# Shorter filler products at the start, and one mantissa moved behind an activation, in a Fourier mixing and hardswish MLP kernel

## The chip, the core and the metric

The kernel runs on one core of a Trainium2 chip. The metric is the device time of one execution in microseconds (us). The engines are named as the profile names them: PE is TensorE (matrix products), PEld its weight loads, DVE is VectorE, ACT is ScalarE, POOL is GpSimd and SP is SyncE, which issues DMAs.

## The reference

```python
def _attn_ref(x):                       # x: (8, 3008, 256)
    X = np.fft.fft(x, axis=1)
    X = np.fft.fft(X, axis=2)
    return X.real.astype(np.float32)

def _moe_ref(x, w_in, w_out):           # x: (24064, 256), w_in: (256, 2048), w_out: (2048, 256)
    h = x @ w_in
    relu6 = np.clip(h + 3.0, 0.0, 6.0)
    g = h * relu6 / 6.0
    return (g @ w_out).astype(np.float32)
```

The input x is float32, the weights are float64. The real part of a two-dimensional Fourier transform of each of 8 batches goes, flattened to 24064 rows, through a two-layer MLP with the hardswish activation.

## The kernel before

**The long part.** The transform along the sequence (3008 = 47 x 64) is done in two stages, and the transform along the 256 columns is folded into `w_in`, so that the MLP's first products (L558, tiles `u` and `v`) finish the transform too. Work goes by pair of batches, chunk of rows and eight steps (`fc`) in each chunk. A step has the first products (`mlp1`), an activation on DVE and ACT (`activate`: two `s` on L567, a sum and a difference on L577 and L579, `relu` on ACT, and two gates on L609), and the second products with the mixed `w_out` (L653, or L633 in the first chunk). The loop at L1156 issues step s + 2's first products before step s's second ones; what has to be prepared for later chunks is put beside the steps by a table written out by hand. Each engine works through its own instructions in the order in which the program issues them.

**The start.** Before the loop three things are made on the core. The weights arrive as float64 and are converted by hand in 16 pieces of 128x512: `exponent_a` on ACT takes the exponent bytes of a piece into `PM`, `exponent_b` turns them into a power of two by two float16 products with a small table in `FI` (L779), `exponent_c` on ACT finishes that, `mantissa` on DVE makes the fraction by two instructions (L787 and L792), and `join` multiplies the two (L803 or L809). `fold_w_in` (L834) multiplies converted pieces of `w_in` by the column table `C`. In the same stretch the first batch is transformed in its first stage: DVE folds four tiles and their mirrored partners (`fold_columns`, L204 and L205), and PE multiplies each tile and partner by a table of 47 rows and 64 columns (`unit_columns` L342, `unit_middle` L328), on four quarters of the array at a time. Results go by ACT (the last by DVE, L354) to SBUF and on.

**The filler.** Before any data is there, `keep_awake(4)` multiplies a tile of zeros (`Z`) by a tile of ones, both set by DVE. Each float32 product is issued as two passes of 128x512, each with a weight load. It is the first work of PE; behind it come the two exponent products of piece 0 (L779), which wait for `PM`, then `keep_awake(1)` and `keep_awake(1, TB)`, whose results nobody reads either, and then the first tile's `unit_columns`.

**The first eight steps.** While the pieces are still being converted, the loop runs `first_steps` and `second_steps` in turn. In `second_steps(3)`, the fourth step, pieces 10 to 13 are in work: piece 13's `exponent_a` is followed by its `head_b`, which is its `mantissa` (and, for pieces 4 to 9 alone, the issue of a later load), then by half of the second products, then by `mlp1` of the next step, whose activation follows on DVE. Piece 13's `join` comes in the step after that.

Of the kernel before, what the change touches and what calls it, by code (L numbers as in the profile page):

```python
# [7 lines left out]
F32 = mybir.dt.float32  # L8
# [4 lines left out]
F16 = mybir.dt.float16  # L13
# [45 lines left out]
def kernel(  # L59
# [10 lines left out]
    nc = tc.nc  # L70
    P = nc.NUM_PARTITIONS
# [16 lines left out]
    TB = KC * N2  # L88
# [18 lines left out]
    ps_d = ctx.enter_context(tc.tile_pool(name="ps_d", bufs=1, space=PSUM))  # L107
# [20 lines left out]
    ones = consts.tile([P, P], F32, name="ones")  # L128
# [416 lines left out]
    def mlp1(ch, fc):  # L545
        activate(ch, fc, *mlp1_products(ch, fc))
# [64 lines left out]
    def combine(ch, fc):  # L611
        a = ch.a[fc][:].rearrange("p m f n -> p (m f) n")[:, :, 0:ch.n]
        c = cpool.tile([P, 4, TB], F32, tag="c", name="c")
        cn = c[:, :, 0:ch.n]

        eng = nc.vector if ch.final and fc == NF - 1 else nc.gpsimd
        add(cn[:, 0:2], a[:, 2:3].to_broadcast([P, 2, ch.n]), a[:, 3::-3], eng)
        add(cn[:, 2], cn[:, 0], a[:, 0], eng)
        add(cn[:, 3], a[:, 1], cn[:, 2], eng)
        ch.c[fc] = cn  # L620
# [6 lines left out]
    def mlp2_first(ch, fc, halves=(0, 1)):  # L627
        a = ch.a[fc]
        for h in halves:
            if fc == 0:  # L630
                ch.acc[h] = ps_a.tile([P, 2, TB], F32, tag="acc", name="acc")
            for f in range(2):
                nc.tensor.matmul(ch.acc[h][:], G[:, (B11, B12, B21, B22)[2 * f + h], fc, :], a[:, :, f],  # L633
                                 start=(fc == 0 and f == 0), stop=(fc == NF - 1 and f == 1))
            if fc == NF - 1:
                if h == 0:
                    ch.r = epool.tile([P, 2, 2, TB], F32, tag="r", name="r")
                for m in range(2):
                    nc.scalar.mul(ch.r[:, m, h], ch.acc[h][:, m], (1 - 2 * m) / WS)
# [99 lines left out]
    PIECES = [q for j in range(NWO) for q in [("in", j, 0), ("in", j, 1), ("out", j, 0), ("out", j, 1)]]  # L739
# [6 lines left out]
    def load_w(j, queue=nc.gpsimd, clear=None):  # L746
        kind, n, i = PIECES[j]

        pool, tag, bufs = (wpool, "st", 2) if j in STRAIGHT else (spool, "t", None) if j in (2, 3) else (xpool, "x", None)
        st = pool.tile([P, 2 * WB], I32, tag=tag, bufs=bufs, name="st")  # L750
        if clear:
            clear.memset(st[0:1, 0:1], 0)
        o = st[:].bitcast(moe_w_in.dtype).rearrange("p (c j) -> p c j", c=2)
        fs = slice((2 * n + i) * 2 * P, (2 * n + i + 1) * 2 * P)
        if kind == "in":
            queue.dma_start(out=o, in_=moe_w_in[:, fs].rearrange("(c p) f -> p c f", p=P))
        else:
            queue.dma_start(out=o, in_=moe_w_out[fs, :].rearrange("(c p) d -> p c d", p=P))
        raw[j] = st

    def exponent_a(j, signs=range(2)):
        top = raw[j][:].bitcast(I16).rearrange("p (n four) -> p n four", four=4)[:, :, 3]
        for i in signs:
            low = PM[j % len(PM)][:, i].bitcast(U8).rearrange("p (n two) -> p n two", two=2)[:, :, 0]
            nc.scalar.activation(low, top, AF.Identity, bias=bias[:, i:i + 1], scale=(1 - 2 * i) / 16.0)

    def exponent_b(j):
        pm = [PM[j % len(PM)][:, i].bitcast(F16) for i in range(2)]
        if j in (0, 1, 4):
            exs[j] = ps_h.tile([P, WB], F32, tag="uv", name="ex")[:]  # L770
        elif j in (2, 5):
            exs[j] = ps_d.tile([P, WB], F32, tag="d", name="ex")[:]
        elif j % 2 == 0:
            exs[j] = bank([P, WB], "ex")[:]
        else:

            exs[j] = spare[1 if j % 4 == 1 or j == 3 else 0][:].rearrange("p i n -> p (i n)")
        for i in range(2):
            nc.tensor.matmul(exs[j], E[:, i], pm[i], start=(i == 0), stop=(i == 1))  # L779

    def exponent_c(j):
        nc.scalar.activation(exs[j].bitcast(I32), exs[j], AF.Identity, scale=2.0 ** 23)
# [11 lines left out]
    def mantissa(j):  # L794
        mantissa_high(j)
        mantissa_low(j)

    def join(j):
        kind, n, i = PIECES[j]
        frac, ex = fracs.pop(j), exs.pop(j)  # L800
        if kind == "in":
            o = wpool.tile([P, WB], F32, tag="wi", bufs=4, name="wi")
            nc.vector.tensor_tensor(o[:], frac, ex, op=AL.mult)  # L803
            w[PIECES[j]] = o[:]
            return

        for h, g in enumerate((slice(B11, B21 + 1), slice(B12, B22 + 1, B22 - B12))):
            f, e = (t.rearrange("p (c q h e) -> h p c q e", c=2, h=2, e=DH)[h] for t in (frac, ex))
            nc.vector.tensor_tensor(G[:, g, 2 * n + i, :].rearrange("p c (q e) -> p c q e", e=DH), f, e, op=AL.mult)  # L809
# [47 lines left out]
    def keep_awake(n, w=2 * TB):  # L857
        ps = ps_d.tile([P, 2 * TB], F32, tag="d", name="awake")
        for i in range(n):
            nc.tensor.matmul(ps[:, 0:w], ones[:], Z[:, 0:w], start=True, stop=True)  # L860

    Z = spool.tile([P, 2 * TB], F32, tag="s", name="Z")
    nc.vector.memset(Z[:], 0.0)
    nc.vector.memset(ones[:], 1.0)
    keep_awake(4)
    hb = halves[0]
    load_w(0, nc.sync)
    nc.scalar.dma_start(out=F[:], in_=c_stage1[:, 0:8 * PB])
# [27 lines left out]
    def head(j):  # L896
        exponent_a(j)
        head_b(j)

    def head_b(j):  # L900
        mantissa(j)
        if j in NEXT:
            load_w(NEXT[j])
# [6 lines left out]
    def see(x):  # L910
        nc.gpsimd.tensor_copy(seen[:], x)
# [9 lines left out]
    for k, t in enumerate(units[1:], 1):  # L921
        m = FIRST[k // 2]
        i = m + (1 - k % 2) * NM
# [138 lines left out]
    def chunk(s):  # L1062
        p, ck, fc = steps[s]
        return chunks[p][ck], fc
# [57 lines left out]
    def second_steps(s):  # L1122
        j = 2 * s + 4
        if j - 2 < len(PIECES):
            if s == 1:
                see(WN[:, 6:7])
            head_b(j)
            join(j)
            head_b(j + 1)
            if s == 1:  # L1130
                mlp2_first(*chunk(s), halves=(0,))
                exponent_b(j + 1)
            exponent_c(j + 1)
            if j + 2 < len(PIECES):
                head(j + 2)
            join(j + 1)
            if j + 3 < len(PIECES):
                exponent_a(j + 3)
                if s > 1:
                    head_b(j + 3)  # L1140
            if s > 1:
                mlp2_first(*chunk(s), halves=(0,))
            mlp1(*chunk(s + 1))
            if s == 1:
                head_b(j + 3)
            return
        mlp1(*chunk(s + 1))
        combine(*chunk(s + 1))
        mlp2_first(*chunk(s), halves=(0,))
        mlp1(*chunk(s + 2))  # L1150
        mlp2_first(*chunk(s), halves=(1,))
# [134 lines left out]
```

## Time and profile before

| what | value |
|---|---|
| median of 3 timed runs | 1929.74 us (1929.35 to 1929.78) |
| the profiled execution | 1935.54 us |
| its span, first to last instruction | 1933.8 us |
| busy: PE, PEld, DVE, ACT, POOL | 1921.0, 1658.5, 1429.4, 678.2, 1447.9 us |
| mean granted clock of PE | 0.994 |
| DMA moved | 99.78 MB, mean 52 GB/s |

The profile is one execution. Times in its timeline count from the span's start. A row of the timeline has the start, the length, engine, line, operation, what is written and read, the shape and the count; in brackets stands the idle time of the engine ahead of it and what ended it. The granted clock is a share of full speed, and is known only from the first recorded change of it.

### The profile page before, as it was taken

The page shows a single profiled execution, that of the slowest core. Times are in us where ns is not written, and L with a number is a line of the kernel's source. Part 1 is how long each engine was busy: PE and PEld are TensorE (multiplying, and loading weights), DVE is VectorE, ACT ScalarE, POOL GpSimd, SP SyncE. Part 2 cuts the span into 40 slices and gives each one's busy share as a digit, 9 for nine tenths or more (in the row PEclk, how much of TensorE's full clock was granted, in tenths as well). Part 3 has the DMA queues.
Part 4 walks back from the last instruction along what each step waited for, and adds up shares of the span by engine and source line. Part 5 has one row for each costly group of instructions (what it writes and reads, how often), then busy time and mean ns, then how long its engine had stood idle before and what let it go on. Part 6 is the DMA issues. An engine that isn't in the chain of part 4 may idle for free.

```text
span 1933.8 us, 28339 instructions
## 1 busy us (share of the span) xinstructions
PE 1921.0 (99%) x9404; PEld 1658.5 (86%) x9404; DVE 1429.4 (74%) x2755; ACT 678.2 (35%) x1165; POOL 1447.9 (75%) x1661
## 2 busy tenths in 40 slices
PE   9999999999999999999999999999999999999998
PEld 6688888888988888888898888888899888888887
DVE  6877767777777777777787777777778777777777
ACT  5533333333333333333333333333333333333332
POOL 5597888896678877887678877878666667666765
PEclk8999999999999999999999999999999999999999
DMA  7532232311112222121111221222110101101000
GB/s 248 154 105 51 55 78 71 70 44 36 34 33 60 67 55 55 44 53 33 34 36 49 53 56 44 51 53 51 36 28 20 29 17 26 32 15 28 18 21 20
DMA packets 155353, 99.78 MB, mean 52 GB/s; under 512 B 121839, under 2 KB 135514, under 8 KB 155206
## 3 DMA queue, kind: packets, MB, share of 16 engines
q1 hardware_dynamic: 142966, 61.15, 12.9%
q0 software_dynamic: 10992, 36.24, 6.5%
q8 instruction: 74, 1.21, 0.3%
q10 hardware_dynamic: 1248, 0.59, 0.1%
q14 instruction: 73, 0.60, 0.1%
HBM read 61.44 MB, written 36.79 MB: 51 GB/s over the span
## 4 chain that ended last, share of the span: by engine, by line
PE 95%; DVE 3%; ACT 1%; issue 0%; DVEq 0%; ACTq 0%
PE acc L653 56%; PE v L558 16%; PE u L558 16%; PE ps L507 2%; PE ps L277 1%; PE acc L633 1%; DVE a L609 1%; PE ps L342 1%; DVE s L567 1%; ACT t L606 1%; PE awake L860 0%; DVE o L714 0%; DVE u L590 0%; PE wps L834 0%; PE ps L468 0%
## 5 line engine op out<-in xcount | busy, mean ns | idle before, releaser
L623 POOL TENSOR_TENSOR c<-a 128x512 f32<-128x512 f32 (+1 forms) x375 | 469.5, 1252 | 358.2 <-PE acc L653 304.5
L653 PE MATMUL acc<-c,G 128*128 128x256 f32 (+1 forms) x3008 | 697.2, 375 | 0.0
L606 ACT ACTIVATE t<-u,half 128x512 f32<-128x512 f32 (+1 forms) x384 | 260.7, 679 | 1141.9 <-DVE u L577 1059.3
L653 PEld LDWEIGHTS acc<-c,G 128*128 128x128 f32 x3008 | 565.2, 190 | 71.6 <-POOL c L623 0.4
L567 DVE SCALAR_TENSOR_TENSOR s<-qn,WN,u 128x256 f32<-128x256 f32 (+1 forms) x768 | 330.3, 471 | 339.6 <-PE u L558 335.7
L653 PE MATMUL acc<-a,G 128*128 128x256 f32 (+1 forms) x2256 | 541.6, 376 | 0.0
L653 PEld LDWEIGHTS acc<-a,G 128*128 128x128 f32 x2256 | 421.1, 189 | 73.5 <-issue 20.1
L558 PE MATMUL v<-q,W 127*128 127x256 f32 (+1 forms) x1536 | 389.3, 375 | 2.1 <-DVE a L609 2.1
L558 PE MATMUL u<-q,W 128*128 128x256 f32 (+1 forms) x1536 | 388.0, 375 | 0.0
L609 DVE SCALAR_TENSOR_TENSOR a<-t,u 128x512 f32<-128x512 f32 (+2 forms) x448 | 264.0, 601 | 101.7 <-ACT t L606 98.3
L558 PEld LDWEIGHTS v<-q,W 127*128 127x128 f32 x1536 | 287.9, 190 | 42.8 <-DVE a L609 2.8
L558 PEld LDWEIGHTS u<-q,W 128*128 128x128 f32 x1536 | 285.9, 190 | 37.1 <-issue 2.6
L623 POOL TENSOR_TENSOR c<-a,c 128x256 f32<-128x256 f32 (+1 forms) x375 | 269.1, 717 | 29.4
L623 POOL TENSOR_TENSOR c<-c,a 128x256 f32<-128x256 f32 (+1 forms) x375 | 269.0, 717 | 29.4
L577 DVE TENSOR_TENSOR u<-s,v 128x512 f32<-128x512 f32 x352 | 245.0, 696 | 38.1 <-DVE s L567 1.9
L609 DVE SCALAR_TENSOR_TENSOR a<-t,v 128x512 f32<-128x512 f32 (+1 forms) x480 | 263.8, 566 | 0.3 <-ACT t L606 0.3
L606 ACT ACTIVATE t<-v,half 128x512 f32<-128x512 f32 (+1 forms) x384 | 260.7, 679 | 0.3 <-issue 0.3
L579 DVE TENSOR_TENSOR v<-v,s 128x512 f32<-128x512 f32 x352 | 243.9, 693 | 0.0
L623 POOL TENSOR_TENSOR r<-w,e 128x256 f32<-128x256 f32 (+1 forms) x92 | 88.8, 987 | 3.6
L663 ACT ACTIVATE e<-acc 128x512 f32<-128x512 f32 (+2 forms) x184 | 83.4, 544 | 0.0
L714 DVE STREAM_TRANSPOSE o<-r 128x256 f32<-128x256 f32 (+1 forms) x192 | 72.5, 415 | 0.2
L623 POOL TENSOR_TENSOR w<-w,e 128x512 f32<-128x512 f32 (+1 forms) x46 | 57.6, 1252 | 3.6
(129 smaller groups left out, 795.1 us busy)
## 6 DMA issues: line engine op xcount, KB each, us to landing
out_dram<-o SPq DMA_DIRECT2D x744, 32.0 KB
g<-zd SPq DMA_DIRECT2D x42, 256.0 KB
zd<-z SPq DMA_DIRECT2D x48, 192.0 KB
xt<-in_x_dram POOLq DMA_DIRECT2D x21, 256.0 KB
qn<-qd SPq DMA_DIRECT2D x16, 256.0 KB
xt<-in_x_dram POOLq DMA_DIRECT2D x17, 192.0 KB
st<-in_moe_w_in_dram POOLq DMA_DIRECT2D x6, 512.0 KB
st<-in_moe_w_out_dram POOLq DMA_DIRECT2D x6, 512.0 KB
```

What stands on the lines that cost most here:

```text
L277: nc.tensor.matmul(ps[b][h * PB:(h + 1) * PB, 0:n], F[rows(b), 0:PB], y[rows(b), 2 * h:2 * h + n], start=True, stop=not last, skip_group_c ...
L507: nc.tensor.matmul(ps[:, blk, u * P:n].rearrange("p (b k) -> p b k", b=2), g[:, kk, blk * (P + 1):blk * (P + 1) + P], T[:, :, gr, blk, kk, ...
L558: nc.tensor.matmul(ps[:, i, 0:nq], W1[r, blk, f * P:(f + 1) * P], q[r, blk, of:of + nq], start=True, stop=True)
L567: nc.vector.scalar_tensor_tensor(s[:, i, 0:nq], qn[:, of:of + nq], WN[:, f:f + 1], u[:, i, 0:nq], op0=AL.mult, op1=AL.add)
L577: nc.vector.tensor_tensor(u[:], s[:], v[:], op=AL.add)
L579: nc.vector.tensor_tensor(v[:], v[:], s[:], op=AL.subtract)
L606: nc.scalar.activation(t, h, AF.Relu, bias=half[:], scale=scale)
L609: nc.vector.scalar_tensor_tensor(dst, t, 1.0, h, op0=AL.min, op1=AL.mult)
L623: (eng or nc.gpsimd).tensor_tensor(out, in0, in1, op=AL.add)
L653: nc.tensor.matmul(ch.acc[i // 2][:, i % 2, 0:ch.n], G[:, i, fc, :], mv, start=(fc == 0 and i % 2 == 0), stop=(fc == NF - 1), skip_group_c ...
L663: nc.scalar.mul(ch.e[:, k:i + 1, 0:ch.n], ch.acc[i // 2][:, 0:i + 1 - k, 0:ch.n], 1.0 / WS)
L714: nc.vector.transpose(o[:, 0:n // DH, h], ch.r[:, m, h, 0:n].rearrange("p (j i) -> p j i", i=DH))
```

## The change

The first `keep_awake(4)` (8 passes of 128x512 in float32, 16 instructions with their weight loads) is replaced by 56 products of 64 columns, with the same tiles read as float16 (112 instructions with their weight loads). The two later fillers stay as they are. In `second_steps` the `head_b(j + 3)` is issued behind `mlp1` in every step that has one; in effect that moves it in the fourth step alone (s = 3, piece 13), as it stood there already for s = 1, and later steps have no such piece. On DVE the two instructions of piece 13's mantissa change places with the six of the activation; on the other engines the order is as before, but for the filler.

```diff
@@ -862,7 +862,9 @@
     Z = spool.tile([P, 2 * TB], F32, tag="s", name="Z")
     nc.vector.memset(Z[:], 0.0)
     nc.vector.memset(ones[:], 1.0)
-    keep_awake(4)
+    awake = ps_d.tile([P, TB // 4], F32, tag="d", name="awake")
+    for i in range(56):
+        nc.tensor.matmul(awake[:], ones[:].bitcast(F16)[:, 0:P], Z[:].bitcast(F16)[:, 0:TB // 4], start=True, stop=True)
     hb = halves[0]
     load_w(0, nc.sync)
@@ -1136,12 +1138,10 @@
             join(j + 1)
             if j + 3 < len(PIECES):
                 exponent_a(j + 3)
-                if s > 1:
-                    head_b(j + 3)
             if s > 1:
                 mlp2_first(*chunk(s), halves=(0,))
             mlp1(*chunk(s + 1))
-            if s == 1:
+            if j + 3 < len(PIECES):
                 head_b(j + 3)
             return
```

## Prediction

> **What bounds the kernel now.** I read the page's head first, then the chain of waits, then the windows of the first 40 us, since the first part of the change is the first thing that TensorE does.
>
> ```profile
> span 1933.8 us, 28339 instructions
> PE 1921.0 (99%) x9404; PEld 1658.5 (86%) x9404; DVE 1429.4 (74%) x2755; ACT 678.2 (35%) x1165; POOL 1447.9 (75%) x1661
> PEclk8999999999999999999999999999999999999999
> PE 95%; DVE 3%; ACT 1%; issue 0%; DVEq 0%; ACTq 0%
> ```
>
> TensorE is busy 99% of the span and is 95% of the chain that ends last. What it loses is lost in idle time or at a low clock, and the clock row has one slice below 9: the first. The windows (columns: stretch, length, busy time and count for PE, PEld, DVE, ACT, POOL, then granted clock, DMA share, GB/s) place it:
>
> ```profile
> 13.00:14.00 1.00, 0.46 (x5) 0.42 (x9) 0.96 (x2) 0.27 (x3) 0.63 (x3) 0.80 0.78 258
> 14.00:26.00 12.00, 12.00 (x173) 10.63 (x166) 5.32 (x11) 5.26 (x14) 5.50 (x10) 0.50 0.79 261
> 26.00:30.00 4.00, 4.00 (x14) 2.62 (x10) 1.29 (x2) 1.40 (x4) 2.53 (x4) 0.50 0.18 38
> 30.00:31.00 1.00, 1.00 (x4) 0.49 (x3) 0.70 (x2) 1.00 (x3) 1.00 (x3) 0.67 0.87 176
> 80.00:1900.00 1820.00, 1818.68 (x8813) 1582.56 (x8812) 1341.01 (x2552) 620.62 (x1066) 1387.69 (x1570) 1.00 0.18 45
> ```
>
> A mean of 0.80 in 13 to 14 means that the clock halved at 13.6; 0.67 in 30 to 31 means that it came back at 30.66. For 17.1 us TensorE was fully busy at half clock, worth 8.5 us at most. From 80 to 1900 us it idles 1.3 us of 1820, so a microsecond gained or lost ahead of that arrives whole at the end. The waits of TensorE up to 110 us (total, times, longest) are the other places to gain:
>
> ```profile
> PE awake L860 <- DVE ones L864: 1.6, 1, 1.6
> PE v L558 <- DVE a L609: 1.2, 2, 1.0
> PE ps L342 <- issue: 0.8, 1, 0.8
> ```
>
> **Part 1, the first filler.** In the timeline of TensorE's weight loads, one load goes with each product, so the distance between starts is the cost of a product:
>
> ```profile
> 5.18 0.33 PEld L860 LDWEIGHTS awake<-Z,ones 128*128 128x128 f32 x1 [0.52 <-issue]
> 6.03 0.33 PEld L860 LDWEIGHTS awake<-Z,ones 128*128 128x128 f32 x1 [0.52 <-issue]
> 6.83 0.19 PEld L860 LDWEIGHTS awake<-Z,ones 128*128 128x128 f32 x1 [0.47 <-issue]
> 7.26 0.10 PEld L779 LDWEIGHTS <-FI 128*128 128x128 f16 x1 [0.24 <-issue]
> 27.90 0.15 PEld L779 LDWEIGHTS <-FI 128*128 128x128 f16 x1
> 28.33 0.15 PEld L779 LDWEIGHTS <-FI 128*128 128x128 f16 x1 [0.28 <-issue]
> ```
>
> A float32 pass of 512 columns costs 0.85 us up to 6.8 and 0.43 us behind it. So the chip starts at half clock too (the page prints 1.00 there, as nothing had been recorded yet), and the rise came at 6.8, after 5.2 us of unbroken products of 128 rows. The second rise, at 30.66, came 4.2 us after the second such run began; the run of 47-row products from 14 to 26 raised nothing, though it filled TensorE:
>
> ```profile
> 1.60 6.25 PE L860 MATMUL awake<-Z,ones 128*128 128x512 f32 x8 [1.60 <-DVE ones L864]
> 7.69 0.59 PE L779 MATMUL ex<-PM,FI 128*128 128x512 f16 x2
> 8.12 1.78 PE L860 MATMUL awake<-Z,ones 128*128 128x512 f32 x4
> 9.83 1.09 PE L342 MATMUL ps<-xt,F 47*64 47x258 f32 x16
> 26.46 2.07 PE L834 MATMUL wps<-wi,C 128*128 128x256 f32 x4
> 6.42 1.43 ACT L765 ACTIVATE PM<-st,bias 128x512 uint8<-128x512 int16 x2
> ```
>
> Removed: eight passes from 1.60 to 7.69. Added: 56 loads and 56 products of 64 columns in float16, not in the trace. Low bound: a float16 product of 512 columns takes 28.33 - 27.90 = 0.43 us at half clock, so 64 columns take 0.053 and 56 of them 3.0 us. High bound: the load's 0.15 and the product one after the other, 0.20, 11.4 us. Which end is right is told by two groups with a load for every product:
>
> ```profile
> L460 PE MATMUL ps<-TF,g 128*128 128x128 f32 x8 | 1.1, 275 | 0.0
> L847 PE MATMUL spare<-last_row,W 128*128 128x1 f32 x8 | 0.9, 240 | 0.0
> ```
>
> Eight products of 128 columns take 1.1 us busy and eight of one column 0.9: the columns nearly vanish beside the loads, so loads and products overlap. I take 3.0 us: the filler ends at 4.6 instead of 7.7, and 3.0 us of work is less than the 4.2 and 5.2 that came ahead of the two rises. I therefore expect no rise at 6.8.
>
> [...]
>
> Behind the filler TensorE waits for the exponent bytes: ACT ends the two halves at 7.1 and 7.85, as now. At half clock: second exponent product 7.9 to 8.3, two filler passes of 0.85 to 10.0, some 0.2 us for the wait on its own result (8.12 to 9.83 now holds 1.29 us of passes and so 0.4 us of two waits), two of 0.43 to 11.1. The first unit products start at 11.15 instead of 9.83, +1.3 us. Those of the first tile take 1.1 us at full clock with the small ones beside them (the row at 9.83), its partner's as many passes some 0.9 without, so together 4.0 at half: 15.1. The next tile starts now at 13.54:
>
> ```profile
> 13.54 2.33 PE L342 MATMUL ps<-xt,F 47*64 47x254 f32 x17 [0.77 <-issue]
> 12.80 0.68 DVE L204 TENSOR_TENSOR xt<-xt 111x508 f32<-111x508 f32 x1
> 13.52 0.69 DVE L205 SCALAR_TENSOR_TENSOR xt<-xt 111x508 f32<-111x508 f32 x1
> 18.55 0.42 DVE L205 SCALAR_TENSOR_TENSOR xt<-xt 111x254 f32<-111x254 f32 x1
> 26.24 0.69 DVE L354 COPY z<-ps 128x512 f32<-128x512 f32 x1 [6.33 <-PE ps L342]
> ```
>
> So the chain that is at half clock in both moves by 15.1 - 13.6 = **+1.5 us**; DVE's folds have been done since 18.97 and DVE idles 6.33 us for TensorE, so nothing hides it. [...]
>
> **Part 2, the mantissa.** In the fourth step the two mantissa instructions of piece 13 stand ahead of the activation:
>
> ```profile
> 68.92 0.42 DVE L787 TENSOR_SCALAR top<-st 128x512 int32<-128x512 int32 x1
> 69.38 0.69 DVE L792 SCALAR_TENSOR_TENSOR top<-st,top 128x512 f32<-128x512 uint32 x1
> 69.98 0.87 DVE L567 SCALAR_TENSOR_TENSOR s<-qn,WN,u 128x256 f32<-128x256 f32 x2
> 72.41 0.69 DVE L609 SCALAR_TENSOR_TENSOR a<-t,u 128x512 f32<-128x512 f32 x1 [0.15 <-ACT t L606]
> 71.16 1.03 PE L558 MATMUL u<-q,W 128*128 128x256 f32 x4
> 73.15 1.13 PE L558 MATMUL v<-q,W 127*128 127x256 f32 x4 [0.96 <-DVE a L609]
> ```
>
> From 68.92 to 69.98 is 1.06 us. The activation moves ahead by that; its first gate ends at 72.04, not 73.10, and the v products that waited 0.96 us start at 72.1, about 0.1 behind the u products. Gain **0.9 us**. Late next: the joins of pieces 12 and 13 have DVE's same sum of work ahead of them, so they stay within 0.2 us, and no load stands behind this mantissa (piece 13 frees none). If the joins delay a fold, the gain falls to nothing, and below nothing by the 0.2 us.
>
> **Sum.** The profiled execution took 1935.54 us (1933.8 of span, 1.7 around it), so a profiled one of the change would take 1935.5 + 1.5 - 0.9 = 1936.1. The median of the timed runs is 1929.74, 5.8 lower. With 1.3 us of idle time between 80 and 1900 the 5.8 can only lie in the start, and only the half-clock stage is large enough: at full clock the units end some 1.5 us behind DVE's folds, at 20.5 instead of 26.5, 6.0 less. So I take it that timed runs of the kernel before keep the clock there (without the 0.77 us stall), and that the change loses it: 1929.74 + 5.8 + 1.5 - 0.9 = **1936.1 us**, +0.33%; own range 1932.5 to 1938.5, the ends being the 0.9 of the rise, 0.9 of the mantissa, and a kernel before that keeps only part of the clock.
>
> **Rivals.**
> First, the clock rises at about 10.2, from 7.2 to 10.2 of products of 128 rows. By the rows above, 3.0 us with a gap of 0.3 was never enough. Then the units start 0.9 us late at full clock, catch up with DVE (0.68 + 0.69 a tile against 1.0 here), and only the mantissa counts: 1928.8. [...]
> Second, the pairs take about 0.11 us (56 in 6.1 us, between the two bounds), the filler ends where it did, and part 1 does nothing: 1928.8 again.
> Third, the timed runs of before lose the clock as the profile does, and the 5.8 us are elsewhere: 1929.74 + 0.6 = 1930.3.
> Fourth, on the other side: the stall before 13.54, which no wait explains, comes by TensorE's count of instructions (it ends at the 128th), and with 96 more ahead it falls under the filler. If before does lose the clock in timed runs because of that hole, and the change has the clock at 10.2, it keeps it: 6.0 us less, and 0.9: 1922.8. It decides only if both hold; for it speaks the hole just before the drop at 13.6, against it the 5.8 us.
>
> **How the numbers follow.** A measurement of this kernel can tell about 0.2%, 3.9 us. Forecast 0.53; first rival 0.13, second 0.07, third 0.10, fourth 0.17. So slower 0.53, same 0.30, faster 0.17. The range leaves out the fourth rival and the uppermost tail: 1927.5 to 1938.5.
>
> **What would show it.** Right: first filler ending near 4.7, loads still 0.15 us (float16) and 0.33 us (float32) from 7 to 11, first unit products near 11, folds' evictions on DVE near 28, no wait of v on a gate near 73. Wrong: a rise of the clock at 6.8 or 10.2, or a filler that lasts until 7 us; or half clock gone from 14 to 26.

## The result, and the profile after

| kernel | median of the timed runs | lowest to highest | profiled execution, span |
|---|---|---|---|
| before, measured beside it | 1929.67 us (20 runs) | 1929.03 to 1930.35 | 1935.54 us, 1933.8 us |
| changed | 1932.78 us (20 runs) | 1929.49 to 1936.79 | 1935.85 us, 1934.1 us |

The ratio is 1.0019 with a 95% interval of 1.0012 to 1.0027: slower by about 0.2%. (The ratio is not the quotient of the two medians, which is 1.0016.) The twenty times of the changed kernel form groups: eight at 1929.5 to 1930.6, three at 1932.3 to 1933.2 and nine at 1935.9 to 1936.8. The median falls between them, into a gap where few executions lie.

The head of the page of the changed kernel (span, busy times, the row of the granted clock):

```profile
span 1934.1 us, 28436 instructions
PE 1918.6 (99%) x9452; PEld 1658.3 (86%) x9452; DVE 1430.9 (74%) x2755; ACT 677.1 (35%) x1165; POOL 1446.7 (75%) x1661
PEclk7999999999999999999999999999999999999999
```

Again only the first slice of the clock row is below 9. The timeline of TensorE there:

```profile
1.61 3.17 PE L867 MATMUL awake<-Z,ones 128*128 128x64 f16 x56 [1.61 <-DVE ones L864]
7.22 0.38 PE L779 MATMUL ex<-PM,FI 128*128 128x512 f16 x1 [2.45 <-ACT PM L765]
7.88 0.38 PE L779 MATMUL ex<-PM,FI 128*128 128x512 f16 x1 [0.28 <-ACT PM L765]
8.09 2.75 PE L860 MATMUL awake<-Z,ones 128*128 128x512 f32 x4
10.77 1.99 PE L342 MATMUL ps<-xt,F 47*64 47x258 f32 x16
26.77 2.07 PE L834 MATMUL wps<-wi,C 128*128 128x256 f32 x4
```

The 56 pairs (each a weight load and its product) take 3.17 us, 2.5 us of idle time follow, and the first products behind the units (the 47-row products of L342 and L328) start at 26.77 (26.46 before). The windows of the same trace, cut where the records have the clock change (columns as in the prediction):

```profile
1.70:5.11 3.41, 3.08 (x56) 2.91 (x56) 2.82 (x4) 2.94 (x3) 2.73 (x5) 1.00 0.92 275
5.11:8.52 3.41, 1.02 (x4) 0.57 (x4) 2.69 (x6) 2.92 (x5) 2.62 (x3) 1.00 1.00 366
8.52:11.93 3.41, 3.35 (x16) 1.29 (x18) 3.31 (x6) 0.35 (x1) 2.68 (x3) 0.50 0.91 317
11.93:25.59 13.66, 13.66 (x199) 10.67 (x196) 7.71 (x15) 4.68 (x15) 6.97 (x15) 0.50 0.79 272
25.59:29.00 3.41, 3.41 (x26) 2.33 (x19) 1.29 (x2) 1.55 (x3) 1.23 (x3) 0.50 0.15 33
```

The clock rose at 5.11, fell at 8.52 and rose again at 29.00. (Ahead of the first record the page prints 1.00, but the pairs run at half clock there: they start 0.0534 us apart, and an eighth of the 0.43 us that 512 columns of float16 took at half clock before is 0.054.) From the first to the second change is 3.41 us, from there to the third 20.48, six times as much; and before, 13.60 to 30.66, 17.06 us, was five times. So I read TensorE's rows in windows of 3.41 us that end at the changes; the records give only the changes. The window up to 5.11 was busy for 3.08 of 3.41 us, 90%, and the clock rose at its end; the next was busy for 30%, and it fell; then products of 128 rows filled 66% (8.52 to 10.77) and the 47-row units the rest, and it stayed low, and from there on units alone filled every window until 25.59. The last window, 25.59 to 29.00, is mixed as well: units until 26.8 and products of 128 rows for 65%, and the clock rose at its end.

The mantissa in the fourth step on DVE, what POOL does at that time (L222 to L231, a fold of tiles for the next half batch), and the waits of TensorE up to 110 us that bear on it:

```profile
72.62 1.01 DVE L787 TENSOR_SCALAR top<-st 128x512 int32<-128x512 int32 x1
73.66 1.64 DVE L792 SCALAR_TENSOR_TENSOR top<-st,top 128x512 f32<-128x512 uint32 x1
75.22 0.67 DVE L803 TENSOR_TENSOR wi<-top,ex 128x512 f32<-128x512 f32 x1
76.42 0.86 DVE L567 SCALAR_TENSOR_TENSOR s<-qn,WN,u 128x256 f32<-128x256 f32 x2
```

```profile
72.08 1.27 POOL L222 TENSOR_TENSOR y<-xt 111x508 f32<-111x508 f32 x1
73.30 1.45 POOL L223 TENSOR_TENSOR y<-xt 111x508 f32<-111x508 f32 x1
74.72 0.65 POOL L224 TENSOR_TENSOR y<-xt 111x6 f32<-111x6 f32 x1
```

```profile
PE spare L779 <- ACT W L842: 1.2, 1, 1.2
PE v L558 <- DVE a L609: 0.3, 1, 0.3
```

The 0.96 us wait of the `v` products is gone. But L787 and L792 take 2.65 us instead of 1.11, and each ends shortly after the POOL instruction that it started under (L787 at 73.63 and L222 at 73.35, L792 at 75.30 and L223 at 74.75). The joins, the next activation and ACT behind it are late by that, and the exponent products (L779) now wait 1.25 us for ACT's copy, in place of the 0.96:

```profile
81.80 0.59 PE L779 MATMUL spare<-PM,FI 128*128 128x512 f16 x2 [1.25 <-ACT W L842]
```

In the kernel before the same fold of POOL ran at nearly the same time, beside the activation's gates (L609, from 72.41) and the joins (L803), which took 0.68 to 0.69 us each there:

```profile
72.23 1.26 POOL L222 TENSOR_TENSOR y<-xt 111x508 f32<-111x508 f32 x1
73.45 1.27 POOL L223 TENSOR_TENSOR y<-xt 111x508 f32<-111x508 f32 x1
74.67 0.22 POOL L224 TENSOR_TENSOR y<-xt 111x6 f32<-111x6 f32 x1
```

So the fold runs where it ran before; the move has put the mantissa beside it.

What the mantissa costs can be read apart from the clock, as the length from the first to the last L633 product (first and last start in the view of that line; first the kernel before, then the changed one):

```profile
L633 PE MATMUL acc<-a,G x64: 590/592/667, 40.7 to 98.8; 128*128 128x512 f32 x64
```

```profile
L633 PE MATMUL acc<-a,G x64: 590/592/667, 40.8 to 99.1; 128*128 128x512 f32 x64
```

58.1 against 58.3 us by these rounded figures; by single instructions 58.05 against 58.38. So 0.33 us lost, not 0.9 gained, and it is the whole difference of the two spans (1933.8 and 1934.1): up to the first L633 the two executions are level to 0.03 us.

### The profile page after: what moved, and what is told of

It reads as the page before. It is cut to its first block, busy times and chain, and to the rows that moved or that the text cites. A ratio compares the mean times of both kernels' runs of the same rounds, so it can differ in the third digit from the quotient of the medians.

```text
span 1934.1 us, 28436 instructions
## 1 busy us (share of the span) xinstructions
PE 1918.6 (99%) x9452; PEld 1658.3 (86%) x9452; DVE 1430.9 (74%) x2755; ACT 677.1 (35%) x1165; POOL 1446.7 (75%) x1661
## 4 chain that ended last, share of the span: by engine, by line
PE 94%; DVE 3%; ACT 1%; POOL 1%; issue 0%; DMA 0%; ACTq 0%; DVEq 0%; POOLq 0%
PE acc L653 56%; PE v L558 16%; PE u L558 16%; PE ps L507 2%; PE ps L277 1%; PE ps L342 1%; PE acc L633 1%; DVE a L609 1%; DVE s L567 1%; ACT t L606 0%; ACT PM L765 0%; POOL c L623 0%; DVE o L714 0%; PE ps L468 0%; DVE u L590 0%
## 5 line engine op out<-in xcount | busy, mean ns | idle before, releaser
L609 DVE SCALAR_TENSOR_TENSOR a<-t,u 128x512 f32<-128x512 f32 (+2 forms) x448 | 264.2, 602 | 101.5 <-ACT t L606 97.1
L609 DVE SCALAR_TENSOR_TENSOR a<-t,v 128x512 f32<-128x512 f32 (+1 forms) x480 | 263.6, 566 | 0.3 <-ACT t L606 0.3
```

The source lines that it names most:

```text
L609: nc.vector.scalar_tensor_tensor(dst, t, 1.0, h, op0=AL.min, op1=AL.mult)
```

## The experiments

Every kernel ran for five rounds with the kernel before on the same chip, unless said otherwise. "Near 1936" stands for 1935 to 1937.3 us, the group in which every profiled execution had lost the clock until TensorE had left the units.

**1. The mantissa alone.** The kernel before, with only this:

```diff
             if j + 3 < len(PIECES):
                 exponent_a(j + 3)
-                if s > 1:
-                    head_b(j + 3)
...
-            if s == 1:
+            if j + 3 < len(PIECES):
                 head_b(j + 3)
```

> Only the mantissa of piece 13 is moved; the first filler stays at eight float32 passes. Window theory (the clock rises only behind a stretch of 3.41 us on a grid that does not start with the kernel, and the filler of 3.0 us fills such a stretch in some executions only): the single times lie as close together as those of the kernel before (within about 1.5 us), and the median is 0.9 us lower, 1928.8, with the v products of the step near 73 us no longer waiting. Rival (the mantissa's move has a part in the added time or in the scatter): the median is above 1929.7 or the times spread over several us.

Measured: 1930.04 us (1929.59 to 1933.59, 11 runs) against 1929.60, ratio 1.0007 (0.9998 to 1.0016). None is near 1936, but three lie at 1933.1 to 1933.6, so they are not as close together as expected; two of the 33 times of the kernel before in that session, 1931.7 and 1933.0, stand out likewise. L787 and L792 take 1.02 and 1.64 us here too, and the view of L633:

```profile
L633 PE MATMUL acc<-a,G x64: 590/592/667, 34.8 to 93.2; 128*128 128x512 f32 x64
```

58.4 us, as in the changed kernel. This execution keeps its clock from 6.2 us on (span 1928.1), and is 5.9 us ahead of the profiled execution of before at the first L633 (34.8 for 40.7). So the 5.8 us between profile and median do lie in the start, and the move of the mantissa makes this stretch 0.3 us longer, where I had expected 0.9 less.

**2. The filler alone.** The other half of the change (the hunk of `awake` in the diff above), the mantissa left where it was.

> Only the first filler is changed to the 56 float16 products; the mantissa stays ahead of the activation. Window theory: the same scatter as with the whole change, times from about 1930.4 to 1937.7, each group 0.9 us above that of the whole change, median 2 to 8 us above the kernel before. Rival (the mantissa's move takes part): the scatter is gone or much smaller.

Measured: 1929.99 us (1928.75 to 1935.53, 11 runs), ratio 1.0003 (0.9994 to 1.0012). One of 11 near 1936, the profiled one, with the clock up at 5.16, down at 8.57 and up at 29.05; three more at 1931.7 to 1932.7. The filler alone brings the loss of the clock, but far more seldom in this sample than I had expected. With the mantissa in front the length from the first to the last L633 is 58.0 us (40.8 to 98.8).

**3. The same count, twice the columns.** The changed kernel with 128 columns in each filler product, so 112 instructions as in the change, and about twice the time:

```diff
-    awake = ps_d.tile([P, TB // 4], F32, tag="d", name="awake")
+    awake = ps_d.tile([P, TB // 2], F32, tag="d", name="awake")
     for i in range(56):
-        nc.tensor.matmul(awake[:], ones[:].bitcast(F16)[:, 0:P], Z[:].bitcast(F16)[:, 0:TB // 4], start=True, stop=True)
+        nc.tensor.matmul(awake[:], ones[:].bitcast(F16)[:, 0:P], Z[:].bitcast(F16)[:, 0:TB // 2], start=True, stop=True)
```

> As the whole change, but each of the 56 float16 products has 128 columns instead of 64: again 112 instructions, now 0.107 us each at half clock, about 6 us in all, so the filler ends where the float32 one did. Window theory (length decides): the single times close up to within about 1.5 us and the median is 1928.8, that of the mantissa alone. Rival (the number of instructions or the float16 type decides): times scatter from 1929.5 to 1936.8 as with the whole change.

Measured: 1930.12 us (1929.50 to 1930.46, 11 runs), ratio 1.0000 (0.9991 to 1.0009), none near 1936.

```profile
1.60 5.46 PE L867 MATMUL awake<-Z,ones 128*128 128x128 f16 x56 [1.60 <-DVE ones L864]
9.82 1.09 PE L342 MATMUL ps<-xt,F 47*64 47x258 f32 x16
```

The units start at 9.82 at full clock. Neither float16 nor the count of instructions lost the clock by itself here. The median is not the 1928.8 that I had from the mantissa's gain, since that did not come.

**4. Few instructions, short.** The mantissa moved, and `keep_awake(2)` for the first `keep_awake(4)`: 4 float32 passes, 3.4 us at half clock.

> The mantissa moved, and the first filler is float32 as before but with four passes of 128x512 instead of eight (3.4 us). Window theory (length decides): the times scatter as with the whole change, some near 1929 and some near 1936, though there are only 8 instructions and no float16. Rival (instruction count or type decides): the times stay within 1.5 us, median 1928.8.

Measured: 1930.37 us (1929.47 to 1936.81, 11 runs), ratio 1.0010 (1.0001 to 1.0019); two near 1936 and one at 1932.4. So shortness does it with 8 instructions as well. Its profiled execution shows what was enough to keep the clock there (records: a rise at 5.88 and no fall):

```profile
2.47:5.88 3.41, 2.92 (x4) 0.78 (x3) 2.68 (x4) 3.40 (x4) 2.58 (x5) 1.00 0.98 323
5.88:9.30 3.42, 1.72 (x5) 0.59 (x5) 3.17 (x7) 2.52 (x4) 2.65 (x3) 1.00 0.99 377
```

The clock rose behind a window busy for 85% (2.92 of 3.41 us), and stayed behind one busy for 50% (1.72 of 3.42).

**5. POOL's fold held back.** The mantissa moved, the long filler kept, and one element copied on POOL, so that its fold (L222 and on) starts only behind piece 13's mantissa (`made` takes that mantissa's result; "..." marks what is left out here):

```diff
+    def wait_made():
+        nc.gpsimd.tensor_copy(mark[0:1, 0:1], made[0][0:1, 0:1])
...
                 for part in range(2):
+                    if k == 0 and part == 1:
+                        put(5, wait_made)
                     put((4, 6, 11, 14)[k] + part, fold_half, hb, m, part, nc.gpsimd)
```

> The kernel before with the mantissa of piece 13 behind the activation (as in the change), and in addition one POOL copy of a single element of that mantissa's result, placed ahead of the fold part L222 to L231, so that this fold starts only when the mantissa is done. Theory (POOL's folds held up the moved mantissa): L787 and L792 take 0.42 and 0.69 us again instead of 1.01 and 1.64, the next activation starts on DVE near 74.9 and not 76.4, the wait of TensorE for ACT's copy of spare (1.25 us) shrinks to about nothing, and with the v wait gone too the time is about 0.9 us below the kernel before: ratio 0.9995, 1928.7 us. The fold itself starts 1.7 us later and the gathers behind it too, which have several us to spare. Rival (the place behind the activation itself makes the mantissa late, POOL or not): L792 stays near 1.6 us, time about 0.4 us above the kernel before, 1930.0. Second rival (the fold's delay is on the path): the mantissa is short again, but a wait for the folded half appears on TensorE behind 85 us and the time is 1930 or more.

Measured: 1930.14 us (1929.45 to 1933.91, 11 runs), ratio 1.0003 (0.9994 to 1.0012). DVE, POOL and TensorE (this execution runs some 5 us ahead of that of the changed kernel):

```profile
67.27 0.42 DVE L787 TENSOR_SCALAR top<-st 128x512 int32<-128x512 int32 x1
67.73 0.69 DVE L792 SCALAR_TENSOR_TENSOR top<-st,top 128x512 f32<-128x512 uint32 x1
80.25 0.87 DVE L567 SCALAR_TENSOR_TENSOR s<-qn,WN,u 128x256 f32<-128x256 f32 x2 [3.11 <-DMA WN<-W]
```

```profile
68.48 0.17 POOL L800 COPY mark<-top 1x1 f32<-1x1 f32 x1 [1.69 <-DVE top L792]
68.62 1.25 POOL L222 TENSOR_TENSOR y<-xt 111x508 f32<-111x508 f32 x1
```

```profile
83.42 1.13 PE L558 MATMUL v<-q,W 127*128 127x256 f32 x4 [1.76 <-DVE a L609]
```

With POOL out of the way the mantissa takes 0.42 and 0.69 us again, in the same place behind the activation: POOL's fold was what held it up. The exponent products no longer wait. But the gathers behind the fold are late as well (issued at 72.9 and 74.25), the last small transfer of `W`'s last row into `WN`, issued at 76.8, lands at 80.2, and an activation waits 3.11 us for it. (The gathers' own landing is not in this trace; in experiment 1 they took 5.8 and 6.1 us from issue, which would be 78.7 and 80.3 here.) That gives a new wait of 1.76 us for `v`, and the length from the first to the last L633 is 59.0 us (35.4 to 94.4), worse than 58.4. The second rival was right that the delay would come back, though not by the folded half. That the gathers' traffic is what slows the small transfer is argued from their times only.

**6. The same with the float16 filler of experiment 3.**

> The same arrangement of mantissa and POOL's fold, with 56 float16 filler products of 128 columns (112 instructions, about 5.5 us) in place of the four float32 ones. If length is what keeps the clock and the fold is what held up the mantissa: 1928.7 us, all times within 1 us, a rise between 5 and 8.5 us and no fall before the end. If the count of short instructions brings the scatter: times at 1936 again among them.

Measured: 1930.45 us (1929.38 to 1939.52, 11 runs), ratio 1.0006 (0.9997 to 1.0015); nine at 1929.4 to 1930.7, two at 1938.6 and 1939.5. I expected no such times. The profiled execution is one of the two:

```profile
10.65 3.36 PE L868 MATMUL awake<-Z,ones 128*128 128x512 f32 x4 [2.38 <-remote]
```

TensorE stood still from 8.3 to 10.65. The view says "remote", as it finds no instruction that ended the wait. In the changed kernel's trace the load of this filler waits there for TensorE's own exponent product (0.6 us), which in this execution was done by 8.3. The window from 6.64 to 10.06 was therefore busy for only 40%, and the clock was lost until 33.95. The profiled execution of before has a stall without a releaser too, ahead of 13.54 (0.77 us); the long filler did not help against this one. The other of the two was not profiled.

**7. No first filler at all.** The changed kernel without its 56 pairs.

> The changed kernel without its first filler (the two later ones stay): TensorE does nothing until about 7 us. Theory (the clock is judged in windows of 3.4 us whose place differs from execution to execution, and the products from 7.2 to 11.1 fill such a window only where it lies well): most times near 1936.5, some near 1930, median 1936. Rival (only an early filler can raise the clock): all at 1936 to 1938. Rival (the 5.8 us have nothing to do with the clock at the start): 1930 throughout.

Measured: 1930.63 us (1929.41 to 1936.71, 12 runs), ratio 1.0008 (1.0000 to 1.0017). Two near 1936, not most, and a median of 1930.6 where I had 1936: my share was wrong.

```profile
8.27 3.19 PE L860 MATMUL awake<-Z,ones 128*128 128x512 f32 x4
11.39 1.59 PE L342 MATMUL ps<-xt,F 47*64 47x258 f32 x16
21.82 0.44 PE L342 MATMUL ps<-xt,F 47*64 47x127 f32 x5 [1.78 <-issue]
```

With the second filler alone the clock rose, at 12.45 in the records: the window from 9.03 has 69% of 128-row products (to 11.39) and units behind. So the first filler was not needed for the rise; as I read it, the stretch from 7.2 to 11.4 can do it, where a window lies well on it. (Here too there is a stall that no wait explains, 1.78 us, and the clock is low behind it from 22.69 to 26.10.)

**8. The changed kernel again,** for another profiled execution (one run).

> The changed kernel unaltered, for another profiled execution of it. Theory (place of the window): if this execution is near 1930 us, its records show a rise between 5 and 11.5 us that is kept, and the unit products end near 20.5 us and not 26.8; if it is near 1936 us, they show a fall or no rise before 28 us. Rival (the slow executions come from something else than the clock at the start): an execution near 1930 with the half clock from 14 to 26, or one near 1936 without it.

Measured: 1929.93 us, span 1928.2.

```profile
1.61 3.17 PE L867 MATMUL awake<-Z,ones 128*128 128x64 f16 x56 [1.61 <-DVE ones L864]
8.11 2.94 PE L860 MATMUL awake<-Z,ones 128*128 128x512 f32 x4
10.98 1.45 PE L342 MATMUL ps<-xt,F 47*64 47x258 f32 x16
20.25 1.13 PE L834 MATMUL wps<-wi,C 128*128 128x256 f32 x4
```

```profile
4.94:8.35 3.41, 0.83 (x3) 0.57 (x4) 2.82 (x7) 2.92 (x5) 2.80 (x3) 1.00 0.99 368
8.35:11.77 3.42, 3.36 (x12) 1.05 (x14) 3.35 (x6) 0.54 (x1) 2.51 (x4) 0.50 0.86 300
11.77:15.18 3.41, 3.41 (x82) 2.68 (x78) 3.31 (x6) 1.28 (x4) 1.91 (x5) 1.00 0.85 287
```

The same program up to here, the same filler, the same fall; but every window lies 0.17 us earlier. The clock therefore falls earlier too, and the products behind end 0.21 us later (10.98). So the third window holds 77% of 128-row products (8.35 to 10.98) instead of 66%, and the clock rises at 11.77 and stays. The products behind the units start at 20.25, not 26.77, and the span is 5.9 us shorter. This pair of executions carries the explanation.

**9. A longer second filler.** The changed kernel with this:

```diff
-    keep_awake(1)
+    keep_awake(2)
     keep_awake(1, TB)
```

> The changed kernel with one more float32 product (two passes of 128x512) in the second filler, behind the exponent products: the stretch of 128-row products from 7.2 us lasts to about 12.3 at half clock instead of 10.8. Theory (a window of 3.4 us must be filled to about 70%, its place differs, and with the short first filler the second stretch decides): 5 us of stretch holds such a window wherever the grid lies, so the clock is up before 14 us in every execution and no time is near 1936; the units start up to 1.7 us later but catch up with DVE's folds: 1930.0, spread 1 us or so. Rival (the short filler itself, its form or its count, loses the clock): about 4 times in 10 near 1936 as before, median above 1931. Rival (the later start of the units is not hidden): 1931.5, no 1936.

Measured: 1930.05 us (1929.60 to 1933.55, 11 runs), ratio 1.0004 (0.9995 to 1.0013), none near 1936.

```profile
8.25 4.68 PE L860 MATMUL awake<-Z,ones 128*128 128x512 f32 x6
12.86 1.09 PE L342 MATMUL ps<-xt,F 47*64 47x258 f32 x16
21.12 1.13 PE L834 MATMUL wps<-wi,C 128*128 128x256 f32 x4
```

Here the clock came only at 12.56, and the units still end 5.6 us ahead of the changed kernel's 26.77. With the longer stretch the short first filler did no harm in these 11 executions, where the unaltered changed kernel, in the same session on the same chip, was near 1936 in 5 of 11 (experiment 11). That the stretch is long enough for every place of the window is argued.

**10. The longer second filler, and no first one.** The changed kernel without its 56 pairs, and with the edit of experiment 9.

> No first filler at all, and the longer second filler of the run before. Theory: the stretch from 7.2 us lasts to about 13 at half clock, fills a window wherever it lies, and no time is near 1936; units start near 12.5 at full clock and catch up: 1930.0 to 1930.7. Rival (an early rise is needed): 1932 or more throughout, the units ending over 1.5 us later than 20.3.

Measured: 1930.43 us (1930.16 to 1932.19, 11 runs), ratio 1.0008 (0.9999 to 1.0017), none near 1936. The median is as expected, though four times lie at 1931.5 to 1932.2. An early rise was worth little here, since a rise at 13.27 (in its profiled execution) gave a median within 0.5 us of experiment 9's.

**11. The changed kernel a third time.**

> The changed kernel unaltered, once more, for the share of its executions that lose the clock and for another profiled one. Theory: near 1936 in 3 to 6 of 11, near 1930 in the rest but for one or two near 1932 to 1933; median between 1930.3 and 1935.9. If the first sample was a matter of that chip or hour: all near 1930, or all near 1936.

Measured: 1930.42 us (1929.64 to 1937.26, 11 runs), ratio 1.0017 (1.0006 to 1.0027); six at 1929.6 to 1930.4 and five near 1936, the profiled one among these:

```profile
8.27 3.19 PE L860 MATMUL awake<-Z,ones 128*128 128x512 f32 x4
11.39 1.99 PE L342 MATMUL ps<-xt,F 47*64 47x258 f32 x16
27.38 2.07 PE L834 MATMUL wps<-wi,C 128*128 128x256 f32 x4
```

It has no rise before 29.60. Counted back from there its windows end at 5.71, 9.12 and 12.54; the filler fills 73% of the first, and 128-row products 53% of the second and 67% of the third (9.12 to 11.39). Over all 32 executions of the changed kernel, 15 lie at 1929.5 to 1930.6, 3 near 1932 to 1933 and 14 near 1936 (mean 1936.5). Of the 124 times of the kernel before, over all these sessions, none is near 1936; its profiled execution is.

**12. Experiment 9 with the mantissa in front,** so that the two differ in the mantissa alone.

> The short first filler with one more float32 product in the second filler, as in the run before with both, but with piece 13's mantissa ahead of the activation as in the kernel before: the two kernels differ in the mantissa alone. Theory (the moved mantissa costs about 0.4 us, and the second filler makes the short first one harmless): the wait of the v products for a gate (0.93 to 0.96 us) is back, the 1.25 us wait for ACT's copy is gone, L787 and L792 take 0.42 and 0.69 us, and the time is within 0.1 us of the kernel before, with none near 1936: ratio 1.0000. Rival (the 0.5 us over the kernel before come from the fillers): 1930.0 again, ratio 1.0003.

Measured: 1930.13 us (1929.05 to 1932.76, 11 runs) against 1929.25, ratio 1.0005 (0.9996 to 1.0014), none near 1936. I had expected 1.0000. By the times alone the rival, which expected 1930.0 again, stands: with the mantissa in front this kernel is 0.9 us above the kernel before, so its fillers may cost something too, and times like these cannot tell 0.3 us. The trace can:

```profile
L633 PE MATMUL acc<-a,G x64: 590/592/667, 35.4 to 93.4; 128*128 128x512 f32 x64
```

58.0 us, with a wait of 0.9 us for `v` back and that for ACT's copy gone. By single instructions the length is 58.02 to 58.05 us in the three traces with the mantissa in front (the kernel before, experiment 2 and this one). It is 58.38 or 58.39 in seven with the mantissa behind (the changed kernel twice, experiments 1, 4, 7, 9 and 10), 58.59 in experiment 3 and 58.76 in the changed kernel's third; what adds the rest in those two was not followed up. In this execution the start was 0.9 us longer than in experiment 9 (first L633 at 35.4 against 34.5), which hides the gain.

No version here measured faster than the kernel before.

## Why the prediction was right or wrong

**The filler (right).** I took 0.053 us a pair by the columns alone, 3.0 us, end at 4.6. The pairs start 0.0534 us apart and the last starts at 4.53; the weight loads vanish beside the products. The second rival, with 0.11 us a pair, is out: the 56 take 3.0 us and not 6.1.

**No rise at 6.8 (wrong).** The step was that 3.0 us is less than the 4.2 and 5.2 us ahead of the two rises of before, so it cannot raise the clock. The filler did raise it, at 5.11 and 4.94 in two of the three profiled executions, and the clock was full until 8.52 and 8.35; that it was low again behind that is what the forecast had for another reason. As I read it, those lengths were set by where the runs of products began in the window. Worked out from the rows of TensorE, window by window:

| execution | window, us | 128-row products | 47-row units | clock at its end |
|---|---|---|---|---|
| changed, first | 1.70 to 5.11 | 90% | 0 | rises |
| | 5.11 to 8.52 | 30% | 0 | falls |
| | 8.52 to 11.93 | 66% | 32%, behind | stays low |
| | 25.59 to 29.00 | 65% | 35%, ahead | rises |
| changed, second | 8.35 to 11.77 | 77% | 21%, behind | rises |
| changed, third | 2.30 to 5.71 | 73% | 0 | stays low |
| | 9.12 to 12.54 | 67% | 31%, behind | stays low |
| no first filler | 9.03 to 12.45 | 69% | 29%, behind | rises |
| | 19.27 to 22.69 | 13% | 35% | falls |
| two float32 products | 2.47 to 5.88 | 85% | 0 | rises |
| | 5.88 to 9.30 | 50% | 0 | stays high |
| experiment 6 | 6.64 to 10.06 | 40% | 0 | falls |
| | 10.06 to 13.47 | 81% | 0 | stays low |
| before | 10.18 to 13.59 | 0 | 75% | falls |
| experiment 1 | 16.49 to 19.90 | 0 | 92% | stays high |

With 128-row products alone, the clock rose behind windows filled to 85%, 90% and 93% (the last is 1.53 to 4.94 in the second execution), and not behind those of 73% and 81%. Units counted for less: with units alone it never rose, though they filled the four windows from 11.93 to 25.59 to 100%. In windows filled by both, with the units behind, it rose at 69% and 77% of 128-row products and not at 66 to 67%. That is no limit for every mixture: at the end of the stage, with the units ahead and no idle time, it rose at 65 to 67% in three traces (the first and third execution of the change, and experiment 2). What makes the difference is open. Once high, it stayed behind a window with 50% of 128-row products and fell behind those with 24% (4.94 to 8.35 in the second execution), 30% and 40%; with units alone it stayed at 92% and fell at 75%. Every distance between recorded changes of one execution is a whole multiple of 3.41 us (3.41, 10.24, 17.06, 20.48 and 23.89), and the windows' place against the span's start differed from 1.53 to 3.36 us over the profiled executions. That the fill of such a window decides is my reading of these distances and shares; no record says so.

The stretch of 56 pairs filled 90% and 93% of a window in the first two executions, and the clock rose behind it; in the third it filled 73% of one, and the clock did not rise. The window behind, with 2.5 us of idle time, then had 30% and 24%, and the clock fell. Whether the change costs 6 us is decided, as I read it, in the second stretch, from 7.2 to about 11 us, which is just long enough to fill a window in some places and not in others (3.6 to 4.2 us in the changed kernel's three traces). The 33 executions of experiments 9, 10 and 12, where it lasts 5.6 to 5.9 us, have none near 1936.

**That the change loses the clock (half right).** I gave one outcome where there are two, and took the slower one for the median. Executions that lose the clock lie at 1936.5 on the mean, where the forecast was 1936.1; but they are 14 of 32. The one of the others that was profiled does what the first rival says, a rise by the stretch from 7.2 us, at 11.77 and not 10.2. Whether it comes depended on the execution: 77% of the window in this one, 66% and 67% in the two that lost the clock. The shares differ between samples: 9 of 20, 5 of 11, and 1 of 11 with the filler alone. Why is open. So it is luck that the median of the first sample fell into my range of 1932.5 to 1938.5: it lies in the gap between the groups, and the third sample, of the same kernel, has its median at 1930.42, outside.

**The first unit products at 11.15 (about right), +1.5 us (wrong).** They started at 10.77, 10.98 and 11.39 us. But the units ended only 0.3 us later than in the profiled execution of before. The term compared with an execution that had lost 0.77 us, in fact more, in a stall ahead of 13.54 that the changed kernel's executions do not have: the product that starts at 13.58 there starts at 11.85 in experiment 1, whose start is the same program. The stall is an accident of that execution and not a step of the program, and I had counted it as one. Between the two profiled executions I had forecast 0.6 (1.5 less 0.9), and they are 0.31 apart: the 0.3 us at the end of the units is gone at the first L633, and the mantissa adds 0.33. So two wrong terms partly cancelled, and it is in part luck that 1936.1 is close to the executions that lose the clock. The 0.9 us that my range gives to the place of the rise no run shows: from the first product behind the units to the rise it was 4.20 us in the profiled execution of before (26.46 to 30.66) and 2.23 in that of the change (26.77 to 29.00), and with 1.97 us less at half clock the change had made up those 0.3 us by the first L633.

**The mantissa, -0.9 us (wrong).** The wait of 0.96 went, as said. The step that failed is "the joins of pieces 12 and 13 have DVE's same sum of work ahead of them, so they stay within 0.2 us". The sum of work is the same, its time is not: it takes 2.65 us where POOL folds beside it and 1.11 where it does not. The joins came 1.5 us later, a wait of 1.25 us took the place of 0.96, and the term measures +0.33. The row L224 of POOL, 0.65 us for six elements a row (0.22 in before), shows the other side of it. Why the two instructions of the mantissa are held up, and the gates and joins beside the same fold in before were not (0.68 to 0.69 us each), no trace shows. Experiment 5 shows the cause, POOL's fold, apart from the place.

**The 5.8 us in the start (right).** In experiments 1 and 8 the clock is kept or regained there, and the units end 6 us sooner, with the rest alike. This speaks against the third rival, though no timed run of the kernel before was itself profiled. **The fourth rival** is out too: the execution of experiment 1 issues the same instructions up to there as the kernel before and has no such stall, so the count alone does not bring it. (In the records the stall ends at about TensorE's 121st instruction, not the 128th.)

The sign was as forecast. The size, 0.19% for 0.33%, is that of a mix: 14 of 32 executions that lie 6.5 us above the group at 1930 make 2.8 us on the mean, and that group itself lies 0.4 us above the kernel before. The mantissa's 0.33 would about account for that; that it does is argued, since experiment 12 has the mantissa in front and is 0.9 us above the kernel before all the same.

## What to carry to other kernels

A warm-up is sized by what it does over many executions, not by what was enough in one. Here the recorded changes of the clock lie whole multiples of 3.41 us apart, at places that differ from execution to execution (1.53 to 3.36 us against the span's start). A stretch of 3.6 to 4.2 us ahead of the real work left 14 of 32 executions near 1936, and one of 5.6 to 5.9 us none of 33; and behind an early stretch of 3.0 us the clock rose in two of three traces, only to fall behind the 2.5 us of idle time that followed. So make the stretch well longer than that step, without holes, and up against the real work. A stretch of about one step did not cost a bit more each time; it made two kinds of executions, and one profile or one median tells only half. And a piece of DVE work moved by a microsecond is priced by what POOL does at its new place, not by its row at the old one: 2.65 us here, for 1.11.

## What the runs showed of the hardware that I had not expected

- With products at half clock, a float16 load and product of 64 columns takes 0.0534 us, no more than the columns alone (0.054): the load of 128 by 128 weights (the same ones each time) adds nothing that shows.
- A kernel without the first filler (1930.63) was no slower than one with the short one (1932.78, 1930.42). Where the clock was up for one window behind the short filler, the exponent products and the second filler ran faster, ended sooner (10.77 against 11.39 us) and filled less of the window (66% against 69%). That this makes the loss likelier is argued; 2 of 12 against 14 of 32 does not settle it.
- TensorE lost 1.7 to 2.4 us with no wait that the profile explains, in three of the fourteen profiled executions, each of another kernel. The one of experiment 7 ends at 21.82, and experiment 10 has a shorter one, 0.57 us, that ends at 21.84 and, in the records of both, ahead of the same number of TensorE's instructions (the 443rd). Whether TensorE waited for instructions there is not shown. What the stalls are stays open, and so do the times at 1931.5 to 1933.9 that most kernels, that of before included, show now and then.
